# The last 64 of 576 contraction rows: from four tails of two matmuls to one stacked matmul in each of seven block products

## The chip, the cores and the metric

The kernel runs on one core of one Trainium2 chip. The time is that of one execution on the device, in microseconds (us); of several runs the median is given. Its engines work side by side, each through its own list of instructions in order: TensorE (PE, matrix products into PSUM), VectorE (DVE), ScalarE (ACT), GpSimd (POOL) and SyncE (SP, which issues most transfers). Loading a weight into TensorE is a separate instruction (PEld) that runs beside the product before it.

## The reference

A transformer block with two parallel branches on the same normalised input: attention over the positions i, i-2, ..., i-14 with 32 heads of 18 channels, and a dense ReLU layer.

```python
x = A_x                                   # [1, 2048, 576]
xn = (x - mean(x)) / sqrt(var(x) + 1e-5)
# A: q, k, v = split(xn @ wqkv)           # wqkv [576, 1728]
#    logits[w] = q[i] . k[i - 2 w] * 18 ** -0.5, w in 0..7, masked where i - 2 w < 0
#    a = (softmax(logits) . v[i - 2 w]) @ wo       # wo [576, 576]
# B: b = max(xn @ w1, 0) @ w2             # w1 [576, 4608], w2 [4608, 576]
out = x + a + b                           # float32
```

## The kernel before

**Phases and steps.** The 2048 positions are worked in two phases of 1024 (every other position each), a phase in two halves h of 512 and a half in two token blocks j of 256 (`TBN`). The first products (xn times wqkv and w1) go by weight sets of 256 columns: 18 of w1 (kind F) and 7 of wqkv (kind Q) a phase, 50 in all. A step t is one set on one half, so there are 100. Steps 0 to 3 run in a hand-written opening (`OPEN`, lines 34 to 38, run by `opening`, line 1489) as plain products (`classic`, 14 matmuls for each of four output blocks). Steps 4 to 99 (loop at line 1526) run as seven block products by Strassen and Winograd's scheme over a 2 x 2 split of the 512 first contraction rows, of the set's columns and of the half's tokens: `pstep` with P1 to P7 (line 758). The weights' combinations are B11, T1, T2, B21, T3, B22, T4, the tokens' are A-blocks (`XA`) and S1 to S4 (`XS`, made by `s_forms`).

**Precision.** An operand x is split into hi = x rounded to fp32r and lo = x - hi, and a product is hi.hi + hi.lo + lo.hi (`terms`, line 685). A block product over 256 rows is 3 terms x 2 chunks of 128 = 6 matmuls of 128 x 128 by 256 columns.

**The tail.** 576 is 512 + 64 (`DR`). The last 64 rows are no part of the blocks. Their token side `XR` holds hi in partitions 0 to 63 and lo in 64 to 127, their weight side (slot RR of the set) the same 64 rows twice, once as hi and once as lo; `rest` (line 690) issues two matmuls that give all four terms. P2, P3, P4 and P5 each end in one such tail, so a step has 7 x 6 + 4 x 2 = 50 matmuls.

**Weight sets.** `set_make` (line 513) is planned two steps ahead (line 1242) into one of two buffers (`BUF`). It sends four block transfers and two of the rest rows (the same 64 rows into both halves of the partitions) from a copy of the weights in DRAM, lets VectorE form T1 to T4 by four subtractions (c1 to c4 in `TS`), and then makes hi on ScalarE and lo on VectorE in four pairs over two slots each (`parts`, `hi_lo`). `x_load` to `x_done` and `s_forms` do the same for the tokens of the second phase; `xt_direct` for the first, straight from the transposes in PSUM (4 of 128 columns and 1 of 64 for each of 8 row blocks; in the second phase the 64 columns of two row blocks share one transpose, `x_rest`, line 1296).

**Second products.** Between the P's stand visits to the second products (`o_step`, line 951): six matmuls each, three terms by two column parts of 256 and 320, of a hidden block (`H`, in one of `NHB` = 6 buffers `HB`) with w2. The order within a step is P1, P5, P6, P2, P7, P3, P4 with the visits of the F step before dealt out behind P1, P6, P7 and P3. `h_parts` makes hi (ScalarE, with ReLU) and lo (VectorE) of a finished output block; the outputs of Q steps are turned by VectorE into one of `NST` = 4 staging buffers and go to DRAM (`q_out`).

**Attention and order.** VectorE works the attention of four units of eight heads a phase (`attention`, line 1085) as a backlog in the gaps of its other work. The order within an engine is fixed when the program is built, by a planner (`Order`) that estimates durations and gives out the operations of ScalarE and VectorE by due time. GpSimd's instructions are issued as they come: in the first phase the copies of weights into DRAM (`kept_part`, line 478), each behind a one-element copy that waits for the newest hidden block, which paces them; the reciprocal deviation of the normalisation (line 383); the mask (line 1113); and four low parts of the opening (`by_pool` of `hi_lo`).

```python
def rest(bank, s, f, xr):
    w, wd = wset(s), wide(s)
    for e in range(2):
        mm(bank[0:wd], w[:, e, RR, f, 0:wd], xr, False, e == 1)
```

Of the kernel before, what the change touches and what calls it, by code (L numbers as in the profile page):

```python
# [16 lines left out]
P = 128  # L17
NPH = 2
NI = 8
# [10 lines left out]
NHB = 6  # L30
NST = 4
# [3 lines left out]
B0 T2 B1 T3 Q000 K2 F010 F011 T4 Q011 O0101 T5 O0100 S0 O0110 T6  # L35
Q001 K3 O0111 Q010 T7 F100 F101 F110 O1000 S1 O1001 O1010 F111 M2 K4 O1011
Q111 Q100 Q110 O1100 O1101 O1111 Q101 O1110
# [3 lines left out]
T1, B11, T2, B21, T3, B22, T4, RR = range(8)  # L41
B12 = T3

PE, ACT, DVE, SP, PL = "pe", "act", "dve", "sp", "pool"
TAIL = {PE: 0.24, ACT: 0.13, DVE: 0.13}
# [3 lines left out]
class Op:  # L49


    __slots__ = ("eng", "dur", "fn", "after", "due", "end", "lag", "then", "post", "gate")

    def __init__(self, eng, dur, fn, after, due, lag=0.0):
        self.eng, self.dur, self.fn, self.due, self.lag = eng, dur, fn, due, lag
        self.after = [a for a in after if a is not None]
        self.end = None
        self.then = None
        self.post = None
        self.gate = None  # L60


class Order:
# [4 lines left out]
    def __init__(self):  # L68
        self.clk = {PE: 0.0, ACT: 0.0, DVE: 0.0, SP: 0.0, PL: 0.0}
        self.dma = 0.0  # L70
        self.gp = 0.0
        self.wait = {ACT: [], DVE: []}
# [15 lines left out]
    def give(self, op, start):  # L88
# [3 lines left out]
        if op.then:  # L92
            op.then.end = self.gp = max(self.gp, op.end) + op.then.dur
# [26 lines left out]
    def step(self, limit):  # L120
        best = None
        for eng in (ACT, DVE):
# [39 lines left out]

    def later(self, fn, n, after=(), lag=0.0):
# [17 lines left out]
    def keep(self, fn, kb, after=0.0):  # L181

        fn()
        op = Op(PL, 1.0, None, (), 0.0)
        self.clk[PL] = max(self.clk[PL], self.now(), after) + kb / 90.0
        op.end = self.clk[PL] + 3.0
        return op
# [20 lines left out]
def tile_body(ctx: ExitStack, tc: tile.TileContext, x, wqkv, wo, w1, w2, out):  # L208
# [6 lines left out]
    DR = D - KT * P  # L215
    D2 = D // 2
# [54 lines left out]
    mvp = pool("mvp", 6)  # L271
# [16 lines left out]
    XR = [keep.tile([P, 3, TBN], F32R, name=f"xr{h}") for h in range(2)]  # L288
    keep.tile([P, PADS[0]], F32, name="pad0")
    BUF = [keep.tile([P, 2, 2048], F32R, name=f"wset{b}") for b in range(2)]  # L290
    keep.tile([P, PADS[3]], F32, name="pad4")
    HB = [keep.tile([P, 2, TBN], F32R, name=f"hb{b}") for b in range(NHB)]
    WHB = [keep.tile([P, 2, TBN], F32R, name=f"oh{b}") for b in range(2)]
    keep.tile([P, PADS[3]], F32, name="pad5")
# [15 lines left out]
    def wset(s):  # L310
        return BUF[s % 2].rearrange("p e (s k c) -> p e s k c", s=8, k=2)
# [27 lines left out]

    def mm(o, l, r, start, stop):  # L340
        nc.tensor.matmul(o, l, r, start=start, stop=stop, skip_group_check=True)  # L341

    def hi_lo(hi, lo, raw, n, after, slack, behind=(), by_pool=False):

        if by_pool:
            def both():
                copy(hi, raw)
                nc.gpsimd.tensor_tensor(lo, raw, f32(hi), op=ALU.subtract)

            a = act(both, n, after, slack)  # L350
            a.then = b = Op(PL, 0.0055 * n, None, (), 0.0)
            return [a, b]
# [9 lines left out]
    TURNED = [0] * NI  # L362
# [6 lines left out]
    def normalise(i, src, after, slack, by_act=False, alloc=True):  # L369
# [8 lines left out]
        def rest():  # L378
            z["mv"] = mv = mvp.tile([P, 2], F32, name="mv")
            z["r"] = r = mvp.tile([P, 1], F32, name="rstd")  # L380
# [3 lines left out]
            if by_act:  # L384
                z["nm"] = nm = mvp.tile([P, 1], F32, name="nm")
# [14 lines left out]

        if by_act:
            MEANS[i] = b
            NORMED[i] = act(one, D + 200, [b], slack + 1.0)
        else:
            NORMED[i] = dve(two, D // 2 + 100, [b], slack + 1.0)

    def turn_pe(i, pa, pb, after=()):
        def f():
            if pa is not None:
                for k in range(KT):  # L410
                    nc.tensor.transpose(pa[:, k * P : (k + 1) * P], XN[i][:, TURNED[i] + k * P : TURNED[i] + (k + 1) * P], ident)
            if pb is not None:
                nc.tensor.transpose(pb[0:DR, 0:P], XN[i][:, KT * P : D], ident)

        return pe(f, 0.11 * ((KT if pa is not None else 0) + (pb is not None)), [NORMED[i], *after])
# [7 lines left out]
    def xt_direct(i, pa, pb, t, slack, free):  # L423
# [1152 lines left out]
```

## Time and profile before

| | us |
|---|---|
| median of 3 runs | 1114.11 (1112.05 to 1114.87) |
| the profiled execution | 1115.05 |
| its span, first to last instruction | 1113.3 |
| mean granted TensorE clock | 0.999 |

The profile is of one execution. Its page gives busy times, shares of the span and numbers of instructions of each engine; PE's busy time counts pipelined matmuls, so their spacing is read from their starts. The timeline lists runs of like instructions: start, length, engine, line of the kernel, operation, output and inputs, how many, and in brackets the idle time before with what ended it. The windows give busy times by stretch of time. A name such as bk, bkA, pm, po is a PSUM tile; wset is a weight set, xa, xs and xr are the token operands, hb a hidden block, w2t a tile of w2, sn5 and sn2 partial sums, pr, lg, kk, v, qo tiles of attention, spare the target of the pacing copies. Operations of one helper share its line: 341 is a matmul, 338 a VectorE subtraction, 335 a ScalarE copy.

### The profile page before, as it was taken

Reading aid. Unit: us, or ns where it says so; the run is one execution under the profiler, and the core shown is the slowest. Engines: PE = TensorE matmul, PEld = TensorE weight load, DVE = VectorE, ACT = ScalarE, POOL = GpSimd, SP = SyncE. Lnnn points to the kernel's source line nnn. Section 1 sums busy time; section 2 is a strip of 40 time slices with the busy share of each in tenths; the row PEclk is TensorE's granted clock in tenths of the full one; section 3 lists DMA queues with packets and bytes.
Section 4 is the critical chain, followed back from the end, with each engine's and each line's share of the span. In section 5 each row is a group of like instructions: output and inputs, shape, how many; then the busy total and the mean of one; then the engine's idle time right before and its main releaser. Section 6 shows DMA issues by size and latency. Waiting matters only on the chain.

```text
span 1113.3 us, 24046 instructions
## 1 busy us (share of the span) xinstructions
PE 1102.5 (99%) x9047; PEld 1098.6 (99%) x9047; DVE 909.0 (82%) x1749; ACT 756.2 (68%) x1561; POOL 218.3 (20%) x434
## 2 busy tenths in 40 slices
PE   9999999999999999999999999999999999999998
PEld 8998999999999999999999999999999999999998
DVE  7867999999999889955885689989998998997440
ACT  6754666566687677676794565656667766766774
POOL 4132384342554423700210000000000000000000
PEclk9999999999999999999999999999999999999999
DMA  7488488856854552463354745563625415224212
GB/s 218 105 187 199 122 216 192 184 145 169 213 158 127 163 151 84 107 158 92 110 173 93 192 93 110 122 137 83 158 76 117 107 52 141 70 56 86 78 49 86
DMA packets 329862, 144.15 MB, mean 129 GB/s; under 512 B 212097, under 2 KB 310401, under 8 KB 328513
## 3 DMA queue, kind: packets, MB, share of 16 engines
q1 hardware_dynamic: 320176, 115.76, 42.3%
q0 software_dynamic: 9408, 26.55, 8.3%
q8 instruction: 71, 1.16, 0.4%
q14 instruction: 47, 0.38, 0.1%
q10 hardware_dynamic: 160, 0.30, 0.1%
HBM read 118.42 MB, written 50.66 MB: 152 GB/s over the span
## 4 chain that ended last, share of the span: by engine, by line
PE 89%; DVE 3%; SPq 3%; DMA 2%; ACT 2%; issue 1%; POOL 0%; DVEq 0%; ACTq 0%
PE po L341 43%; PE bk L341 26%; PE pm L341 12%; PE bkA L341 7%; SPq L1061 1%; DMA qo<-qd 1%; DMA wset<-w1c 1%; DMA qo<-in_w 0%; DVE pr L1107 0%; DMA wqc<-in_wqkv 0%; DVE sn L338 0%; DVE stg L656 0%; DVE wset L338 0%; ACT x L335 0%; ACT hb L335 0%
## 5 line engine op out<-in xcount | busy, mean ns | idle before, releaser
L341 PE MATMUL po<-w2t,hb 128*128 128x256 f32 (+1 forms) x3456 | 503.5, 292 | 0.1
L341 PEld LDWEIGHTS po<-w2t,hb 128*128 128x128 f32 x3456 | 463.2, 187 | 0.4 <-DVE hb L628 0.4
L335 ACT ACTIVATE x<-po 128x576 f32<-128x576 f32 x286 | 186.3, 651 | 231.5 <-PE po L341 230.6
L341 PE MATMUL bk<-xs,wset 128*128 128x256 f32 (+1 forms) x1584 | 224.0, 277 | 0.6 <-ACT sn L335 0.6
L341 PEld LDWEIGHTS bk<-xs,wset 128*128 128x128 f32 (+1 forms) x1584 | 202.3, 187 | 0.9 <-ACT sn L335 0.8
L335 ACT ACTIVATE po<-x 128x576 f32<-128x576 f32 x286 | 187.0, 654 | 6.0
L481 POOL COPY spare<-hb 1x1 f32<-1x1 f32 x192 | 94.6, 493 | 222.8 <-ACT hb L335 222.8
L341 PE MATMUL bk<-xa,wset 128*128 128x256 f32 (+1 forms) x888 | 125.5, 278 | 1.8 <-DVE sn L338 0.9
L341 PEld LDWEIGHTS bk<-xa,wset 128*128 128x128 f32 (+1 forms) x888 | 113.7, 187 | 2.8 <-DVE sn L338 1.1
L341 PE MATMUL pm<-xs,wset 128*128 128x256 f32 (+1 forms) x720 | 102.2, 277 | 0.3 <-ACT bkA L335 0.3
L338 DVE TENSOR_TENSOR sn<-bk,sn 128x256 f32<-128x256 f32 (+1 forms) x132 | 55.2, 419 | 52.3 <-ACT hb L335 25.3
L341 PEld LDWEIGHTS pm<-xs,wset 128*128 128x128 f32 (+1 forms) x720 | 92.0, 187 | 0.7 <-ACT bkA L335 0.5
L1107 DVE TENSOR_TENSOR pr<-qo,kk 128x1152 f32<-128x1152 f32 x64 | 85.4, 1346 | 7.9 <-DMA qo<-qd 6.9
L1113 POOL TENSOR_SCALAR_AFFINE_SELECT lg<-lg 1x512 f32<-1x512 f32 x8 | 9.6, 1206 | 415.1 <-DVE lg L1110 415.1
L341 PE MATMUL bkA<-xa,wset 128*128 128x256 f32 (+1 forms) x624 | 88.3, 278 | 0.5 <-ACT bkA L335 0.5
L1110 DVE TENSOR_REDUCE lg<-pr 128x64 f32<-128x1152 f32 x64 | 85.3, 1340 | 0.2
L1139 DVE TENSOR_TENSOR pr<-lg,v 128x1152 f32<-128x1152 f32 x64 | 85.2, 1348 | 0.2
L341 PEld LDWEIGHTS bkA<-xa,wset 128*128 128x128 f32 (+1 forms) x624 | 81.4, 187 | 1.0 <-ACT bkA L335 0.7
L335 ACT ACTIVATE hb<-sn 128x256 fp32r<-128x256 f32 x140 | 57.4, 414 | 35.1 <-DVE sn L338 34.6
L341 PE MATMUL bk<-xr,wset 128*128 128x256 f32 (+1 forms) x412 | 80.4, 276 | 0.0
L338 DVE TENSOR_TENSOR wset<-ts,wset 128x512 fp32r<-128x512 f32 (+2 forms) x98 | 65.1, 665 | 10.5 <-ACT wset L335 10.3
L1146 DVE TENSOR_TENSOR pr<-pr 128x288 f32<-128x288 f32 (+1 forms) x128 | 71.4, 597 | 0.0
(156 smaller groups left out, 1551.8 us busy)
## 6 DMA issues: line engine op xcount, KB each, us to landing
w2t<-w2c SPq DMA_DIRECT2D x70, 288.0 KB, 3.3
qd<-stg SPq DMA_DIRECT2D x216, 64.0 KB, 2.0
wset<-w1c SPq DMA_DIRECT2D x105, 128.0 KB, 2.8
w1c<-in_w POOLq DMA_DIRECT2D x68, 144.0 KB, 3.4
w2c<-in_w POOLq DMA_DIRECT2D x68, 144.0 KB, 3.5
out<-x SPq DMA_DIRECT2D x16, 288.0 KB, 2.2
ts<-w1c SPq DMA_DIRECT2D x35, 128.0 KB, 2.7
wset<-w1c SPq DMA_DIRECT2D x70, 64.0 KB, 2.3
```

Of the source, the lines that this page charges most:

```text
L335: nc.scalar.activation(o, i, func)
L338: nc.vector.tensor_tensor(o, a, b, op=op)
L341: nc.tensor.matmul(o, l, r, start=start, stop=stop, skip_group_check=True)
L481: nc.gpsimd.tensor_copy(spare[0:1], f32(LATEST[-1])[0:1, 0:1])
L1061: z = send(lambda: nc.sync.dma_start(o, i.rearrange("i p c -> p i c")), cnt * 2, after)
L1107: nc.vector.tensor_tensor(pr[i], q, window(k, i), op=ALU.mult)
L1110: nc.vector.tensor_reduce(s["lg"][:, i], pr.pop(i).rearrange(heads, d=Dh), axis=AX.X, op=ALU.add)
L1113: nc.gpsimd.affine_select(out=z, in_=z, pattern=[[1, NI], [1, W], [0, HG]], compare_op=ALU.is_ge, fill=-1e9 / scale, base=1 - W, channel_m ...
L1139: nc.vector.tensor_tensor(pr[i].rearrange(heads, d=Dh), e, window(VV[u % 2], i).rearrange(heads, d=Dh), op=ALU.mult)
L1146: nc.vector.tensor_tensor(o, z[:, 0:n], z[:, n : 2 * n], op=ALU.add)
```

## The change

The contraction is split into two halves of 288 rows, each two chunks of 128 and 32 rows (`ROWS`, `XCOL`, `DH`). The 32 rows of a half belong to its blocks and go through the same seven combinations. For one block the four kinds of term are stacked in 128 partitions, 32 each: weights hi, lo, hi, 0 against tokens hi, hi, lo, lo; so one matmul (`rest`) gives the three terms that `terms` gives elsewhere, and each of the seven P's is 7 matmuls (`go`). The opening's plain products take two such matmuls, one of each half.

*Weights.* A set has seven slots of three hi and two lo chunks (`wset`). The rest rows are sent three times into 96 partitions of a new tile `RW`, whose last 32 stay zero (`thrice`), ahead of the blocks. Their combinations (`rsum`) and low parts (`rparts`, on 32 partitions) are done by GpSimd (`less`), their hi by ScalarE. `parts` now covers seven slots of two chunks instead of eight.

*Tokens.* The 2 x 32 columns of a row block are written fourfold by GpSimd (`fours`), turned by two transposes (`turn_rest`), and split by ScalarE and VectorE (`xt_rest`). Their S-forms take four more VectorE subtractions in `s_forms`, and `s_rest` writes them into the place in `XA` of the block that only the plain products read; in the second phase that block isn't made (`x_parts`). `x_rest` makes four transposes instead of one.

*Order and room.* GpSimd's work is given out by the planner like that of ScalarE and VectorE (`gp`, `keep`). The opening's list has the new steps R and another order. Hidden buffers go from 6 to 4, staging buffers from 4 to 3, pads between tiles change with them, and the planning of the last output weights of the first phase (`wo_plan`) moves one step later.

```diff
-NHB = 6
-NST = 4
+NHB = 4
+NST = 3
...
-B0 T2 B1 T3 Q000 K2 F010 F011 T4 Q011 O0101 T5 O0100 S0 O0110 T6
-Q001 K3 O0111 Q010 T7 F100 F101 F110 O1000 S1 O1001 O1010 F111 M2 K4 O1011
-Q111 Q100 Q110 O1100 O1101 O1111 Q101 O1110
+T2 R2 B0 B1 T3 K2 Q000 R3 Q001 T4 T5 F010 Q011 Q010 S0 F011 R4 O0100 R5 T6
+O0110 T7 O0101 R6 K3 R7 O0111 F100 F101 O1000 F111 S1 F110 O1010 M2 K4 Q100
+O1001 O1100 O1011 Q110 Q101 Q111 O1110 O1101 O1111
 """.split()
...
-T1, B11, T2, B21, T3, B22, T4, RR = range(8)
-B12 = T3
...
+B11, B21, B22, T1, T3, T4, T2 = range(7)
+B12 = 7
+C11, C12, C21, C22 = range(4)
+ROWS = (0, 288)
+R3 = 96
...
+    def gp(self, fn, n, after, slack):
+        op = Op(GP_, 0.0022 * n + 0.2, fn, after, self.now() + slack)
+        self.wait[GP_].append(op)
+        return op
...
+    def keep(self, fn, kb, after=(), slack=8.0):
+
+        op = Op(GP_, 0.65, fn, after, self.now() + slack)
+
+        def landed():
+            self.clk[PL] = max(self.clk[PL], op.end) + kb / 90.0
+            op.end = self.clk[PL] + 3.0
...
+        op.post = landed
...
+    DH = DR // 2
+    XCOL = [ROWS[k // 2] + k % 2 * P for k in range(KT)]
...
-        return BUF[s % 2].rearrange("p e (s k c) -> p e s k c", s=8, k=2)
+        z = BUF[s % 2]
+        cut = 21 * P
+        return (
+            z[:, 0:cut].rearrange("p (s k c) -> p s k c", s=7, k=3),
+            z[:, cut:].rearrange("p (s k c) -> p s k c", s=7, k=2),
+        )
...
+    RW = keep.tile([P, 4, P], F32, name="rw")
+    nc.gpsimd.memset(RW[R3:P], 0.0)
+
+    def thrice(src, r0):
+        return src[r0 : r0 + DH][None].to_broadcast([3, DH, src.shape[1]])
...
+    def less(o, a, b):
+        nc.gpsimd.tensor_tensor(o, a, b, op=ALU.subtract)
...
+        def fours():
+            src = XN[i].rearrange("p (q c) -> p q c", q=2)[:, :, 2 * P : 2 * P + DH]
+            nc.gpsimd.tensor_copy(XF[0][:, i % 2], src[:, :, None, :].to_broadcast([P, 2, 4, DH]))
...
+        FOURS[i] = o_.gp(fours, 256, [a, before], slack + 2.0)
...
+    def turn_rest(i, pb, after=()):
+        def f():
+            for q in range(2):
+                z = XF[0][:, i % 2, q].rearrange("p a c -> p (a c)")
+                nc.tensor.transpose(pb[:, q * P : (q + 1) * P], z, ident)
+
+        t = pe(f, 0.11 * 2, [FOURS[i], *after])
...
+    def xt_rest(i, pb, t, slack, free):
+
+        h, j, c = place(i)
...
+        b = slice(2 * j, 2 * j + 2)
+        r1 = act(lambda: copy(XR[h][:, b, c], pr), 256, [t], slack + 1)
+        r2 = dve(lambda: sub(XR[h][DR:P, b, c], pr[DR:P], f32(XR[h][DR:P, b, c])), 256, [r1], slack + 1.5)
+        r3 = act(lambda: copy(RD[h][j][:, :, c], pr), 256, [t, *free], slack + 4)
...
-        r = act(lambda: copy(XR[h][0:DR, 2], RD[h][0:DR]), TBN, RAWR[h], slack + 3)
-        ok.append([r, dve(lambda: sub(XR[h][DR:P, 2], RD[h][0:DR], f32(XR[h][0:DR, 2])), TBN, [r], slack + 3.5)])
...
+        rd = [RD[h][q // 2][:, q % 2] for q in range(4)]
+        b1 = dve(lambda: sub(rd[S1], rd[S3], rd[S1], ALU.add), TBN, [*RAWR[h], *XOK[h, 0], *XOK[h, 1]], slack + 2)
+        b3 = dve(lambda: sub(rd[S3], rd[S2], rd[S3]), TBN, [b1], slack + 2.2)
+        b2 = dve(lambda: sub(rd[S2], rd[S1], rd[S2]), TBN, [b3], slack + 2.4)
+        b4 = dve(lambda: sub(rd[S4], rd[S4], rd[S2]), TBN, [b2], slack + 2.6)
...
+    def s_rest(h, after, slack):
+
+        ops = []
+        for e in (1, 0):
+            raw = RD[h][e]
+            o = XA[h][1][:, e, 0:2]
+            k = act(lambda o=o, raw=raw: copy(o, raw), 512, [RSUM[h], *after], slack)
+            ops += [k, dve(lambda o=o, raw=raw: sub(o[DR:P], raw[DR:P], f32(o[DR:P])), 512, [k], slack + 0.8)]
+            XOK[h, 10 + (S1 if e else S2)] = XOK[h, 10 + (S1 if e else S2)] + ops[-2:]
+        return ops
...
+        for rows in range(2):
+            for v in range(1 if wd == P else 2):
+                if wd == P:
+                    d_, s_ = RW[0:R3, 2 * rows : 2 * rows + 2].rearrange("p s c -> p (s c)"), src_
+                else:
+                    d_, s_ = r[0:R3, 2 * rows + v], src_[:, v * wd : (v + 1) * wd]
+                got["r", rows] = send(
+                    lambda: nc.sync.dma_start(d_, thrice(s_, ROWS[rows] + 2 * P)), 96, [*there, *rw_free[0]], late
...
+        for rows, f, b in ((0, 0, B11), (1, 0, B21), (1, 1, B22), (0, 1, B12)) if fine else (
+            (0, 0, B11), (0, 1, B12), (1, 1, B22), (1, 0, B21)
+        ):
...
+        def rparts(a, b, c, after, slack):
+            n = wd * (b - a)
+            k = act(lambda: copy(hi[:, a:b, 2, 0:wd], r[:, c : c + b - a]), n, after, slack)
+            low = slice(DH, DR)
+            y = [k, o_.gp(
+                lambda: less(hi[low, a:b, 2, 0:wd], r[low, c : c + b - a], f32(hi[low, a:b, 2, 0:wd])), n, [k], slack + 0.5
+            )]
+            for q in range(a, b):
+                ok[q] += y
+            return y
+
+        def rsum(o, a, b, after, slack):
+            return o_.gp(lambda: less(r[:, o], r[:, a], r[:, b]), wd, after, slack)
...
+        rs = 2.0 if fine else 5.0 + y
+        r1 = rparts(B11, B21, 0, [got["r", 0]], rs)
+        e1 = rsum(0, 1, 0, r1, rs + 1.0)
+        r2 = rparts(B21, T1, 2, [got["r", 1]], rs + 0.3)
+        e3 = rsum(1, 3, 1, [e1, got["r", 1]], rs + 1.2)
+        e2 = rsum(3, 3, 0, [e3, *r2], rs + 1.4)
+        e4 = rsum(2, 2, 3, [e2], rs + 1.6)
...
+            r4 = rparts(T1, T2 + 1, 0, [e4], rs + 2)
...
+            parts(T1, T4, tw[:, 0:2], [c1, c3], [], 9 + y)
+            parts(T4, T2 + 1, tw[:, 2:4], [c4], [], 10 + y)
+            parts(B11, B22, z[:, B11:B22], [got[B11], got[B21]], [c1, c4], 11 + y)
+            parts(B22, T1, z[:, B22:T1], [got[B22]], [c2, c3], 12 + y)
+        ts_free[0] = [*ok[T1], *ok[T2]]
+        rw_free[0] = [*r4]
...
-    def rest(bank, s, f, xr):
-        w, wd = wset(s), wide(s)
-        for e in range(2):
-            mm(bank[0:wd], w[:, e, RR, f, 0:wd], xr, False, e == 1)
+    def rest(o, s, b, xr, stop=False):
+        wd = wide(s)
+        mm(o[0:wd], wset(s)[0][:, b, 2, 0:wd], xr, False, stop)
...
+        def go(o, b, xs, xr, start, more):
+            def f():
+                terms(o, slot(m, b), xs, start)
+                rest(o, m, b, xr)
+
+            return pe(f, T7, [*ok[b], *more])
...
-            def f():
-                terms(b3, slot(m, T1), sform(h, S1), True)
-                rest(b3, m, 1, XR[h][:, 1])
-
-            op = pe(f, T8, [*ok[T1], *ok[RR], *XOK[h, 10 + S1], *XOK[h, 1], *BANK[n3]])
+            op = go(b3, T1, sform(h, S1), srem(h, S1), True, [*XOK[h, 10 + S1], *BANK[n3]])
...
-
-            op = pe(f, T8, [*ok[B22], *XOK[h, 10 + S4], *BANK[n3]])
+            op = go(b3, B22, sform(h, S4), srem(h, S4), False, BANK[n3])
...
-        at(TG[2 * m] - 2, 2, wo_plan, m)
+        at(TG[2 * m] - (1 if m == WOLAST[0] else 2), 2, wo_plan, m)
...
+        XIN[i] = [send(lambda: nc.sync.dma_start(XN[i], x_v[1, i]), 295)]
...
-            for z in range(2):
-                copy(rr[h][0:DR, j, z * P : (z + 1) * P], pm[z * DR : (z + 1) * DR, 0:P])
-
-        e = act(out_, TBN + 200, [t], 0.5)
+        t = [turn_rest(i + z, pm[:, 2 * z * P : 2 * (z + 1) * P], BANK["pm"]) for z in range(2)]
+        dst = RD[h][j].rearrange("p q (z c) -> p z q c", z=2)
...
-        XOK[h, j] = hi_lo(XA[h][j][:, 0], XA[h][j][:, 1], z, 1024, RAW[h, j], 1.0)
+        k = slice(2 * j, KT)
+        z = kt4(KR[h][j])[:, k]
+        XOK[h, j] = hi_lo(XA[h][j][:, 0, k], XA[h][j][:, 1, k], z, 1024 >> j, RAW[h, j], 1.0)
...
+    def first_rest(s, raw, after, slack, behind=()):
+        hi = wset(s)[0][:, 0:4, 2]
+        low = slice(DH, DR)
+        k = act(lambda: copy(hi, raw), 512, after, slack)
+        SETREST[s] = [k, o_.gp(lambda: less(hi[low], raw[low], f32(hi[low])), 512, [k, *behind], slack + 0.8)]
```

369 lines of the change are left out of this document (190 added, 179 removed).

## The prediction

> **What bounds the kernel now.** I read the page's engine shares first, then the timeline of TensorE, then the windows of all engines.
>
> ```profile
> span 1113.3 us, 24046 instructions
> PE 1102.5 (99%) x9047; PEld 1098.6 (99%) x9047; DVE 909.0 (82%) x1749; ACT 756.2 (68%) x1561; POOL 218.3 (20%) x434
> ```
>
> TensorE stands idle for 1113.3 - 1102.5 = 10.8 us, start and end included, so the time is the number of its instructions times their spacing. A busy PE need not be PE at its peak, so I take the spacing from starts, in one step of the second phase (from its P1 at 877.01 to the next P1 at 888.94):
>
> ```profile
> 877.01 0.84 PE L341 MATMUL pm<-xa,wset 128*128 128x256 f32 x6
> 877.69 1.72 PE L341 MATMUL po<-w2t,hb 128*128 128x256 f32 x12
> 879.25 0.85 PE L341 MATMUL bk<-xs,wset 128*128 128x256 f32 x6
> 879.93 0.39 PE L341 MATMUL bk<-xr,wset 128*128 128x256 f32 x2
> 880.16 0.84 PE L341 MATMUL pm<-xs,wset 128*128 128x256 f32 x6
> ...
> 888.94 0.84 PE L341 MATMUL bk<-xa,wset 128*128 128x256 f32 x6
> ```
>
> From 877.69 to 879.25 twelve second products take 1.56 us, 0.130 each. From 879.25 to 880.16 six block matmuls and two of the xr tail take 0.91 us, 0.1138 each; the tail's two are no cheaper (0.23 for both). The whole step, 50 x 0.1138 + 48 x 0.130 = 11.93 us, is exactly the distance 888.94 - 877.01: nothing but matmuls is in it.
>
> The second engine is VectorE. Of the 35 windows of 20 us in which attention runs (160 to 480 and 640 to 1020), these are the first, the last and four of the five fullest (the fifth, 260 to 280, has 19.89):
>
> ```profile
> 160.00:180.00 20.00, 20.00 (x171) 20.00 (x171) 19.38 (x40) 10.45 (x21) 9.50 (x25) 1.00 0.83 192
> ...
> 360.00:380.00 20.00, 20.00 (x164) 20.00 (x163) 19.90 (x42) 11.94 (x25) 12.55 (x14) 1.00 0.52 147
> ...
> 440.00:460.00 20.00, 20.00 (x164) 20.00 (x164) 20.00 (x41) 13.25 (x28) 11.42 (x8) 1.00 0.25 69
> ...
> 900.00:920.00 20.00, 20.00 (x165) 20.00 (x165) 19.94 (x38) 13.23 (x28) 0.00 (x0) 1.00 0.23 65
> ...
> 980.00:1000.00 20.00, 20.00 (x164) 20.00 (x163) 19.84 (x34) 12.62 (x27) 0.00 (x0) 1.00 0.21 59
> 1000.00:1020.00 20.00, 20.00 (x165) 20.00 (x164) 18.84 (x44) 14.16 (x28) 0.00 (x0) 1.00 0.29 58
> ```
>
> The columns behind the length are busy times of PE, PEld, DVE, ACT and POOL. DVE has between 0.00 and 0.16 us left in the five fullest windows, and less than 1 us in 15 of the 35; ScalarE and GpSimd have room throughout.
>
> **The change, part by part.** *Matmuls.* Steps 4 to 99 now issue 7 x 7 = 49 instead of 7 x 6 + 4 x 2 = 50; the opening's classic products keep 14. That is 96 fewer at 0.1138: **-10.9 us**, all on the path, provided the stacked operands keep the spacing, as the xr ones did.
>
> *Transposes.* Each of 16 row blocks needs 4 + 2 = 6, 96 in all, where the opening had 5 each and the second phase 4.5: 40 + 36 = 76. The chain of waits prices one:
>
> ```profile
> 536.11 0.44 PE pm L411 x4
> 538.21 0.11 PE pm L1300
> ```
>
> Twenty more at 0.11: **+2.2 us**.
>
> *The weight parts of a set* (48 sets are made by set_make):
>
> ```profile
> L338 DVE TENSOR_TENSOR wset<-wset 128x512 fp32r<-128x512 f32 x90 | 60.5, 684 | 2.3 <-ACT wset L335 2.0
> L338 DVE TENSOR_TENSOR wset<-wset 128x256 fp32r<-128x256 f32 x4 | 1.6, 410 | 0.0
> L335 ACT ACTIVATE wset<-wset 128x512 fp32r<-128x512 f32 x90 | 55.3, 620 | 0.0
> L348 POOL TENSOR_TENSOR wset<-stg,wset 128x256 fp32r<-128x256 f32 x3 | 2.2, 764 | 0.7 <-ACT wset L335 0.7
> L348 POOL TENSOR_TENSOR w2t<-qo,w2t 128x576 fp32r<-128x576 f32 x1 | 1.4, 1424 | 0.0
> ```
>
> DVE's four low parts of 512 become three of 512 and one of 256: 0.684 - 0.410 = 0.27 us less a set, 13 us in all. ScalarE gets three more copies, at most 0.62 each (the 512 row), against 357 us in which it is idle: nothing. GpSimd gets seven instructions: the two POOL rows give (1424 - 764) / 320 = 2.06 ns an element, so about 0.50 for 128, 0.76 for 256, 1.29 for 512; four sums at 0.50 and three low parts of 128, 256 and 512 make **4.55 us a set, 218 us in all**. Low parts on 32 partitions are not in the trace; I give them the full price. GpSimd has 895 us free, so its own time costs nothing. But it shares something with DVE:
>
> ```profile
> L1113 POOL TENSOR_SCALAR_AFFINE_SELECT lg<-lg x8: 1095/1096/1560, 141.2 to 973.7; 1x512 f32<-1x512 f32 x8
> 141.17 1.56 POOL L1113 TENSOR_SCALAR_AFFINE_SELECT lg<-lg 1x512 f32<-1x512 f32 x1 [13.04 <-DVE lg L1110]
> 141.99 1.28 DVE L338 TENSOR_TENSOR w2t<-w2t 128x576 fp32r<-128x576 f32 x1 [0.23 <-ACT w2t L335]
> 793.43 1.50 POOL L1113 TENSOR_SCALAR_AFFINE_SELECT lg<-lg 1x512 f32<-1x512 f32 x1 [111.20 <-DVE lg L1110]
> 793.88 1.25 DVE L338 TENSOR_TENSOR oh<-oh 128x256 fp32r<-128x256 f32 x1
> L338 DVE TENSOR_TENSOR w2t<-w2t 128x576 fp32r<-128x576 f32 x70 | 53.0, 760 | 8.6 <-ACT w2t L335 5.9 <-DMA qd<-stg 2.1
> L338 DVE TENSOR_TENSOR oh<-oh 128x256 fp32r<-128x256 f32 x27 | 12.1, 448 | 0.6 <-ACT oh L335 0.4
> 357.20 6.73 POOL L481 COPY spare<-hb 1x1 f32<-1x1 f32 x1
> L481 POOL COPY spare<-hb x192: 173/175/7105, 45.5 to 477.6; 1x1 f32<-1x1 f32 x192
> ```
>
> Durations behind a colon are least, median and most, in ns. Twice a GpSimd select of 1.1 us met a DVE operation with two inputs in SBUF, and that one took 1.28 instead of 0.76 and 1.25 instead of 0.45: 0.52 + 0.80 us lost, over eight selects, 1.32 / (8 x 1.1) = **15% of GpSimd's time**. The other way a one-element copy of 0.17 us stood for 6.73 us behind an unbroken row of such operations. So a set costs DVE 0.15 x 4.55 - 0.27 = 0.41 us more, with one set in 1113 / 48 = 23 us 0.35 us per window. Only the five fullest windows lack that: 5 x 0.35 - (0.11 + 0.10 + 0.00 + 0.06 + 0.16) = **+1.3 us** on PE. The bounds: no meeting at all gives DVE back 13 us and costs nothing; half of GpSimd's time lost is priced under the rivals. I take the 15%, the only rate that the trace shows.
>
> The Trainium skill, "SBUF — State Buffer", section "Who interferes with whom", speaks against this change: a DVE instruction with two SBUF inputs contends with a GpSimd instruction that reads SBUF, and the second to issue fully blocks until the first is done. By that rule the loss is decided by which engine comes first, and the rows at 141.99, 793.88 and 357.20 agree with it on both sides; how often it happens to seven instructions a set no row shows, and that is what the rivals below are about.
>
> *DMA and queues.* Two rest-row transfers of 96 KB go ahead of the four block transfers on SP, in place of two of 64 KB in the middle; the blocks start two issues later. Sets are made two steps (24 us) ahead, which hides it.
>
> *Buffers.* Hidden buffers go from 6 to 4. In a step of two second-product visits after P3, then P4, P1 and the next visit, P3's output gets its buffer when both visits end (1.56 us), and is read 0.9 + 0.7 + 0.8 us later; ScalarE and DVE need about 0.8 of these 2.4. About 1 us with hand-offs is left: nothing, while DVE is on time. Staging buffers go from 4 to 3, two being filled in a step of 5.6 us or more: nothing.
>
> *Opening and turn between the phases.* The first products wait for GpSimd's low parts:
>
> ```profile
> 8.50 2.21 POOL L348 TENSOR_TENSOR wset<-stg,wset 128x256 fp32r<-128x256 f32 x3 [0.70 <-ACT wset L335]
> 12.59 1.07 PE L341 MATMUL pm<-xa,wset 128*128 128x256 f32 x8
> ```
>
> There it now makes two fourfold copies (at most the 0.76 of the 256 row each), one low part of 512 and two of 256: some 4.3 us from about 8.0, ending at 12.3, where before it ended at 10.7 and the last of them was wanted in the block at 12.59. I take **+0.8 us** for this and the later order; the bounds are +3 and, below nothing, -2.4, if these two stalls go, which hang on where a late attention load falls:
>
> ```profile
> 93.12 0.97 PE L341 MATMUL pm<-xa,wset 128*128 128x256 f32 x6 [1.53 <-DVE sn L338]
> ...
> 95.18 0.97 PE L341 MATMUL bk<-xa,wset 128*128 128x256 f32 x6 [0.85 <-DVE sn L338]
> ```
>
> **Sum**: -10.9 + 2.2 + 1.3 + 0.8 = **-6.6 us**. The profiled execution took 1115.05 us (span 1113.3), giving 1108.4 there; it lies 0.9 above the median of the runs, 1114.11, so the forecast is **1107.5 us**.
>
> **The rivals.** *All of the matmuls arrive.* GpSimd works under reductions and gaps, DVE keeps its 13 us, perhaps the stalls at 93 and 95 go: -8.7 to -11, about 1105. For it: six of eight selects met nothing. Against: DVE's full windows.
>
> *The gain is lost to the shared reads.* At 30% instead of 15% a window owes (0.30 x 4.55 - 0.27) x 0.86 = 0.94 us; 14 of the 35 windows have less, 7.0 us together, so PE pays 14 x 0.94 - 7.0 = 6.2, and -10.9 + 2.2 + 0.8 + 6.2 = -1.7: 1112.4.
>
> *Slower: DVE becomes the bound.* The same place and price, with the rate at 40%: 1.33 us a window, 22 windows short with 16.3 us between them, 12.9 on PE: +5.0, 1119 us, and 1124 at 45%. It decides from about 35%, where the sum is nothing. For it: a waiting GpSimd instruction gets in just when a one-input operation of 0.4 us begins, and holds on into the next one. Against: selects met only twice in eight.
>
> *Sets come late.* The seven GpSimd instructions are a chain with three ScalarE copies between, about 3 us to land and 7 to work in 24 us of room; one wait like the 6.73 fits in, two do not. PE then stands, in order, behind the step's first block that lacks its tail. A set late by 3 us, on five of 48, gives +15 - 6.6: 1122; on two it gives 1113. The median copy waited for nothing (175 ns), which speaks against.
>
> **How the numbers follow.** Forecast 0.34 (1105.5 to 1110.8), all arrives 0.18, lost 0.21, DVE bound 0.13, late sets 0.14 (half of it within 0.3%). A measurement here tells 0.3% from nothing, so faster is below 1110.8 and slower above 1117.5: faster 0.52, same 0.27, slower 0.21. The range 1103 to 1121 takes in all but the far ends of the last two and of the first.
>
> **What would show it.** PE with 8971 instructions and unchanged spacing; xr and xa tails one to a product; GpSimd busy some 430 us. Right: DVE's means for wset, ts and pr a few per cent up, PE idle of 10 to 15 us. Wrong: PE waiting for POOL wset, DVE's two-input means up by a tenth, long waits of PE on DVE sn or ACT hb in the full windows, or a spacing other than 0.1138.

## The result, and the profile after

The changed kernel takes 1186.42 us (median of 4 runs, 1183.51 to 1187.65), the one before 1113.08: **1.065 times as long, 95% interval 1.063 to 1.068**. Forecast was 1107.5. The page of the changed kernel, its first line and the busy times with their counts:

```profile
span 1184.1 us, 24581 instructions
PE 1125.0 (95%) x8971; PEld 1111.8 (94%) x8971; DVE 980.4 (83%) x1763; ACT 796.6 (67%) x1711; POOL 490.7 (41%) x791
```

TensorE issues the 8971 instructions foreseen, 76 fewer than before, yet it is busy 22.5 us longer and idle 1184.1 - 1125.0 = 59.1 us instead of 10.8. VectorE has 14 more instructions and 71 us more to do. Its groups with shapes kept apart (busy time, mean ns of one), in the kernel before:

```profile
L338 DVE TENSOR_TENSOR wset<-ts,wset 128x512 fp32r<-128x512 f32 x90 | 61.2, 680 | 8.5 <-ACT wset L335 8.3
L338 DVE TENSOR_TENSOR ts<-wset,ts 128x256 f32<-128x256 f32 x138 | 55.6, 412 | 6.1 <-DMA wset<-wqc 3.2 <-DMA wset<-w1c 2.3
L338 DVE TENSOR_TENSOR sn<-bk,sn 128x256 f32<-128x256 f32 x126 | 52.7, 419 | 51.5 <-ACT hb L335 25.3 <-PE bk L341 24.0 <-PE pm L1300 1.8
L1146 DVE TENSOR_TENSOR pr<-pr 128x576 f32<-128x576 f32 x64 | 46.3, 747 | 0.0
```

and in the changed one:

```profile
L359 DVE TENSOR_TENSOR wset<-ts,wset 128x512 fp32r<-128x512 f32 x90 | 77.4, 863 | 20.6 <-ACT wset L356 20.1
L359 DVE TENSOR_TENSOR ts<-wset,ts 128x256 f32<-128x256 f32 x138 | 70.3, 522 | 1.1
L359 DVE TENSOR_TENSOR sn<-bk,sn 128x256 f32<-128x256 f32 x126 | 52.3, 415 | 45.0 <-ACT hb L356 26.0 <-PE bk L365 15.5 <-ACT oh L356 2.2
L1236 DVE TENSOR_TENSOR pr<-pr 128x576 f32<-128x576 f32 x64 | 50.3, 809 | 0.0
```

The 512 row of wset<-ts,wset went from 0.680 to 0.863 us, the sums of a set from 0.412 to 0.522, the attention's pr<-pr from 0.747 to 0.809; sn<-bk, which has one input in PSUM, went from 0.419 to 0.415 us. ScalarE has waits that it did not have (total, times, longest):

```profile
ACT wset L356 <- POOL rw L362: 41.2, 20, 5.0
ACT wset L356 <- DMA rw<-w1c: 19.0, 9, 6.2
```

What such a wait does is seen in the timeline of the changed kernel, rows of GpSimd, ScalarE and TensorE together:

```profile
490.42 8.15 POOL L548 COPY spare<-hb 1x1 f32<-1x1 f32 x1
...
499.82 1.72 PE L365 MATMUL po<-w2t,hb 128*128 128x256 f32 x12
...
501.67 0.72 POOL L362 TENSOR_TENSOR wset<-rw,wset 32x128 fp32r<-32x128 f32 x1
...
503.82 1.52 POOL L362 TENSOR_TENSOR rw<-rw 128x128 f32<-128x128 f32 x3
505.37 0.63 ACT L356 ACTIVATE wset<-rw 128x512 fp32r<-128x512 f32 x1 [5.01 <-POOL rw L362]
...
507.95 3.25 PE L365 MATMUL po<-w2t,hb 128*128 128x256 f32 x12 [4.04 <-ACT po L356]
511.00 1.48 PE L365 MATMUL pm<-xs,wset 128*128 128x256 f32 x6
...
513.93 1.73 PE L365 MATMUL po<-w2t,hb 128*128 128x256 f32 x12
```

A pacing copy of one element is blocked for 8.15 us, while VectorE works off a row of instructions with two inputs in SBUF, without a break from 490.18 to 498.43. GpSimd's chain for a set stands behind this copy and two shorter ones, ScalarE stands in order at the copy that needs the chain (5.01 us), behind that copy wait the copies of po, and TensorE loses 4.04 us. Then its twelve second products take 3.25 us instead of 1.72, and the half spacing lasts until some 513.8. The windows show the granted clock, the third figure from the end:

```profile
480.00:500.00 20.00, 20.00 (x165) 20.00 (x164) 19.90 (x37) 12.68 (x29) 10.88 (x7) 1.00 0.23 68
500.00:520.00 20.00, 15.96 (x108) 15.76 (x108) 14.61 (x31) 10.49 (x22) 10.63 (x17) 0.83 0.28 79
```

Counted in TensorE's timeline, the changed kernel has 12 waits of 1.5 us or more (30.9 us together), the one before a single one (1.5 us). Its mean granted clock is 0.985 against 0.999; 0.015 x 1184 gives, as an estimate, 18 us lost to the slow stretches. Not every long wait is followed by one: behind a wait of 3.39 us, at 218.51, the clock stays at 1.00 and six matmuls take 0.97 us.

### The profile page after: what moved, and what is told of

Read it like the earlier page. It is cut to its first block, busy times and chain, and to the rows that moved or that the text cites. A ratio compares the mean times of both kernels' runs of the same rounds, so it can differ in the third digit from the quotient of the medians.

```text
span 1184.1 us, 24581 instructions
## 1 busy us (share of the span) xinstructions
PE 1125.0 (95%) x8971; PEld 1111.8 (94%) x8971; DVE 980.4 (83%) x1763; ACT 796.6 (67%) x1711; POOL 490.7 (41%) x791
## 4 chain that ended last, share of the span: by engine, by line
PE 51%; DVE 21%; POOL 7%; ACT 6%; issue 6%; DMA 5%; SPq 3%; DVEq 0%; POOLq 0%; ACTq 0%
PE po L365 25%; PE bk L365 15%; PE pm L365 7%; PE bkA L365 4%; DVE wset L359 3%; POOL spare L548 2%; DVE ts L359 2%; POOL rw L362 2%; DVE pr L1229 2%; DVE pr L1236 2%; POOL wset L362 2%; DVE hb L722 2%; DVE sn L359 1%; SPq L762 1%; ACT wset L356 1%
## 5 line engine op out<-in xcount | busy, mean ns | idle before, releaser
L365 PE MATMUL po<-w2t,hb 128*128 128x256 f32 (+1 forms) x3456 | 512.0, 295 | 13.5 <-ACT po L356 12.8
L365 PEld LDWEIGHTS po<-w2t,hb 128*128 128x128 f32 x3456 | 469.9, 190 | 15.5 <-ACT po L356 14.1
L362 POOL TENSOR_TENSOR wset<-rw,wset 32x512 fp32r<-32x512 f32 (+2 forms) x145 | 159.6, 1105 | 425.7 <-ACT wset L356 396.0
L365 PE MATMUL bk<-xs,wset 128*128 128x256 f32 (+1 forms) x1584 | 229.6, 282 | 11.2 <-ACT bkA L356 5.9
L365 PE MATMUL bk<-xa,wset 128*128 128x256 f32 (+1 forms) x1140 | 197.9, 280 | 11.5 <-DVE sn L359 8.0
L365 PEld LDWEIGHTS bk<-xa,wset 128*128 128x128 f32 (+1 forms) x1140 | 162.7, 188 | 15.0 <-DVE sn L359 8.3
L362 POOL TENSOR_TENSOR rw<-rw 128x128 f32<-128x128 f32 (+1 forms) x192 | 111.0, 578 | 13.7
L356 ACT ACTIVATE wset<-rw 128x512 fp32r<-128x512 f32 (+2 forms) x145 | 62.7, 443 | 65.7 <-POOL rw L362 41.2
L365 PE MATMUL pm<-xa,wset 128*128 128x256 f32 (+1 forms) x540 | 94.1, 281 | 7.9 <-DVE sn L359 7.8
L359 DVE TENSOR_TENSOR wset<-ts,wset 128x512 fp32r<-128x512 f32 (+2 forms) x98 | 82.4, 844 | 20.6 <-ACT wset L356 20.1
L365 PEld LDWEIGHTS pm<-xa,wset 128*128 128x128 f32 (+1 forms) x540 | 77.3, 189 | 9.3 <-DVE sn L359 9.0
```

The lines of the kernel that those rows point to most:

```text
L356: nc.scalar.activation(o, i, func)
L359: nc.vector.tensor_tensor(o, a, b, op=op)
L362: nc.gpsimd.tensor_tensor(o, a, b, op=ALU.subtract)
```

## The experiments

Rounds share their runs of the kernel before (1112.4 to 1114.1 us); ratios are to it, with their 95% intervals. The runs e2 to e5, e9, e13 and e15 leave out or alter values of the rest rows; they tell times only.

**Buffers, and GpSimd's work as a whole.**

```diff
# e1_buffers: the kernel before
-NHB = 6
-NST = 4
+NHB = 4
+NST = 3
# e2_no_gpsimd: the changed kernel, set_make
-            y = [k, o_.gp(lambda: less(hi[low, ...], r[low, ...], f32(hi[low, ...])), n, [k], slack + 0.5)]
+            y = [k, o_.gp(lambda: None, n, [k], slack + 0.5)]
-            return o_.gp(lambda: less(r[:, o], r[:, a], r[:, b]), wd, after, slack)
+            return o_.gp(lambda: None, wd, after, slack)
```

> The kernel before with four hidden buffers and three staging buffers, nothing else. If the lost buffers cost the time (theory B), a good part of the 73 us between the kernels shows here: 1130 us or more. If the loss lies with GpSimd's work (theories A and C below), 1113 to 1117, as the prediction had it.

> The changed kernel with GpSimd's four sums and its low parts of the rest rows left out of set_make; the planner's order of all other instructions stays. Theory A (VectorE and GpSimd wait for one another at SBUF, VectorE loses some 76 us) and theory C (ScalarE stands, in order, behind copies that wait for GpSimd's chain, and TensorE's granted clock drops after the stalls that follow) both expect the loss to be gone: 1104 to 1112 us, VectorE's 512 row of wset back at about 0.68 us. If buffers, the opening or the new order of the copies cost it (theory B), it stays above 1150.

e1: 1116.28 us, 1.0026 (1.0013 to 1.0038), some 2.6 us. e2: 1125.04 us, 1.0104 (1.0074 to 1.0134). GpSimd's seven instructions a set cost 61.4 of the 73 us, and 11 us above the kernel before remain without them: both theories were only partly right.

**Is it the reads, or the waits on GpSimd?**

```diff
# e3_no_chain: the sums behind the last copy of the rest rows
+        r4 = rparts(T1, T2 + 1, 0, [got["r", 0], got["r", 1]], rs + 2)
+        e1 = rsum(0, 1, 0, [*r1, *r4], rs + 2.2)
...
# e4_no_reads: each `less` of set_make
+        for _ in range(2):
+            nc.gpsimd.memset(o, 0.0)
```

> The same GpSimd instructions as in the changed kernel, but the four sums come behind the last copy of the rest rows, so ScalarE waits for none of them (the terms hold rows that are not summed). Theory C expects most of the loss to be gone: under 1130 us, with VectorE's 512 row still near 0.86. Theory A expects it to stay above 1160, since the shared reads stay.

> Each of GpSimd's subtractions in set_make becomes two fills of the same output, which read nothing, about as long; all waits between GpSimd and ScalarE stay (the rest rows' sums and low parts are not formed). Theory A expects VectorE's 512 row back at about 0.68 us and the time near 1110 to 1120. Theory C in its pure form, a chain that is too long whoever disturbs it, expects above 1150 with VectorE undisturbed; a time between would share the loss out.

e3: 1179.78 us, 1.0585 (1.0564 to 1.0606). e4: 1130.89 us, 1.0158 (1.0129 to 1.0187). VectorE's groups in e4:

```profile
L359 DVE TENSOR_TENSOR wset<-ts,wset 128x512 fp32r<-128x512 f32 x90 | 61.4, 685 | 12.8 <-ACT wset L356 12.2
L359 DVE TENSOR_TENSOR ts<-wset,ts 128x256 f32<-128x256 f32 x138 | 55.3, 414 | 1.5 <-DMA wset<-w1c 0.4
```

With all waits kept and only the reads gone, VectorE is where it was (906 us busy in all) and 55.5 us are back. By e4 against e2, and by e3 against the changed kernel, the waits alone are worth some 6 us. Neither comparison is clean: the fills of e4 take 163 us where the subtractions took 261, so its chain is shorter too, and in e3 VectorE is busy 994 us, 14 more than in the changed kernel. The shared reads are the main cause.

**The reads beside the old kernel, and the same work on VectorE.**

```diff
# e7_load_before: the kernel before, NHB = 5, when the copy of T1's high part is given out
+            nc.gpsimd.tensor_copy(spare[0:1], one)
+            for e in (0, 1, 2, 3):
+                nc.gpsimd.tensor_tensor(d[:, e], d[:, e], d[:, (e + 1) % 4], op=ALU.subtract)
+            for e in (1, 2, 4):
+                nc.gpsimd.tensor_tensor(d[l, 0:e], d[l, 0:e], d[l, 0:e], op=ALU.subtract)
# e8_half_load: the first loop alone
# e6_all_vector: the changed kernel, `sub` given to VectorE in place of `less`
```

> The changed kernel with the four sums and three low parts of a set's rest rows on VectorE in place of GpSimd. By the rows for 256 and 512 elements (0.41 and 0.68 us) that is 4 x 0.25 + 0.25 + 0.41 + 0.68 = 2.3 us a set, 108 us on top of the 906 us of VectorE when GpSimd reads nothing. Theory A: GpSimd's help cost VectorE 74 us of its time, so this comes out no better than the changed kernel, 1170 to 1210, with VectorE's 512 row at 0.68. Theory C (the hand-offs between GpSimd and ScalarE cost it) expects under 1150.

> The kernel before, with five hidden buffers to make room for a scratch tile, and beside each set the same seven GpSimd subtractions (four of 128 x 128, three on 32 rows of 128, 256 and 512) on that tile, behind a one-element copy that paces them; nothing waits for them. Theory A expects the loss without any of the change: 1160 to 1180 us, VectorE's 512 row at 0.8 us or more. If it needs the chain, the new order or the new transfers, 1113 to 1125.

> The same with the four sums of 128 x 128 alone, about 2.0 of the 4.55 us a set. Theory A, with a loss that goes with GpSimd's time: 0.45 of the loss of the full load, 1130 to 1145. If VectorE has that much time to spare before it bounds the kernel, as the prediction's sum by windows had it, less: 1113 to 1120.

e7: 1141.21 us, 1.0253 (1.0232 to 1.0274). e8: 1121.29 us, 1.0077 (1.0055 to 1.0099). e6: 1202.92 us, 1.0804 (1.0786 to 1.0822). The page of e7:

```profile
span 1139.2 us, 24455 instructions
PE 1115.5 (98%) x9047; PEld 1104.4 (97%) x9047; DVE 975.5 (86%) x1749; ACT 752.1 (66%) x1561; POOL 508.0 (45%) x819
```

VectorE loses 975.5 - 909.0 = 66.5 us to 46 x 4.55 = 209 us of such work, 32%; in e8 942.1 - 909.0 = 33 us. Half the load costs 8 us and the whole 28: below the linear share of the smaller load (0.44 x 28 = 12), as one expects of an engine with some time to spare, and just above the second range expected. e7 lies between its two ranges: nearly the same loss of VectorE's time costs the changed kernel 55 (1186.42 - 1130.89). e6 shows that this help of GpSimd is still cheaper than all the work on VectorE, then 1014 us busy, though its loss looks different: 37 of its 90 us are two waits of TensorE, 25.05 and 12.29 us (at 542.51 and 1139.94), while VectorE works off the attention that is left over near the end of each phase.

**What decides between 28 and 55?** Fewer buffers, shorter instructions, the moment:

```diff
# e10_load_buffers: e7 with NHB = 4, NST = 3
# e11_short: low parts of 256 and 512 cut into 128s
+ [less(hi[low, q : q + 1, 2, 0:wd], ...) for q in range(a, b)]
# e12_load_early: e7's load given out ahead of c1, behind the landing of the first block
+        c1.fn = lambda go=c1.fn: (load(z[0:1, B11, 0, 0:1]), go())
# e14_after_sums: ahead of a set's first low part on GpSimd
+                    nc.gpsimd.tensor_copy(spare[0:1], tw[0:1, 2, 0, 0:1])
```

> The kernel before with GpSimd's load as in e7_load_before (1141.21 us), and four hidden and three staging buffers as in the changed kernel (alone they cost 2.6 us). Theory E: fewer buffers are harmless while VectorE is on time and turn its delays into waits of TensorE when it is not, which is why the same load costs 28 us in the old kernel and 55 in the new one: 1155 to 1170. If the buffers only add up: 1141 to 1147.

> The changed kernel with GpSimd's low parts of 256 and 512 elements cut into two and four of 128, the same work in six instructions instead of two. By m1_meeting a subtraction of 512 beside VectorE's row cost VectorE 9.45 / 10 = 0.95 us and one of 128 2.73 / 20 = 0.14, so a set should cost VectorE some 0.5 us less, 23 us in all, and the time 1186 should fall by 10 to 17 us. If the loss goes with GpSimd's time whatever the length, VectorE loses a little more (GpSimd is busy four times 0.24 us longer a set) and the time is 1186 to 1195.

> The kernel before with the load of e7_load_before (1141.21 us), only paced otherwise: it starts when the set's first block has landed, and so beside VectorE's four sums of the set, as in the changed kernel, and not behind the copy that follows them. Theory F (the moment decides: GpSimd holds up the sums from which all copies of the set follow): 1155 us or more, VectorE's ts rows up from 0.46 to over 0.55 us. If only the amount of lost time decides: 1136 to 1146.

> The changed kernel with GpSimd's seven instructions of a set held back, by a one-element copy, until VectorE's four sums of the set are done. Theory F: VectorE's ts rows go back from 0.52 to about 0.42 us and the time from 1186 to under 1170. If the moment does not matter, the chain is only later: 1183 to 1200.

e10: 1146.44 us, 1.0296 (1.0264 to 1.0328): the buffers only add. e11: 1182.1 us, 1.0611 (1.0581 to 1.0641): VectorE's busy time falls from 980.4 to 967.7, half of what was expected, the time by 4 us, hardly clear of the noise; GpSimd is busy 76 us longer (566.3 us), so its chain is longer at the same time. e12: 1138.56 us, 1.0236 (1.021 to 1.0261): the load costs no more at this moment, but it hits VectorE's sums less than was meant (0.487 us, against 0.459 in e7 and 0.522 in the changed kernel). e14: 1209.53 us, 1.0863 (1.0832 to 1.0894): VectorE's sums are back at 0.416 us, but ScalarE now waits 118.9 us for GpSimd's rw, where it waited 41.2. Theory E falls. For F nothing speaks, but neither run settles it: e14 makes the chain later at the same time, and TensorE itself now waits for GpSimd's wset (23 us).

One difference stays visible: e7 has no wait of TensorE of 1.5 us or more and a granted clock of 1.000, the changed kernel 12 and 0.985. In e4, from which the 55 are counted, there are 7 such waits (15.3 us) and a clock of 0.996. So the shared reads bring 15.6 us more of long waits, and by the clocks an estimated 18 - 4.5 = 13 us more of slow stretches: 29 of the 55 us. The 27 left are about what the load costs the kernel before. That is where the difference sits; which part of the new structure lets them grow so long was not settled.

**What remains without GpSimd's work.** Counted by the second products, the same in both kernels, e2 is 9.5 us behind the kernel before at the hundredth, 9 at the 1500th and 17 after the turn between the phases.

```diff
# e5_margin: e2, the planner's landing time of the rest rows
-                    lambda: nc.sync.dma_start(d_, thrice(s_, ROWS[rows] + 2 * P)), 96, [*there, *rw_free[0]], late
+                    ... late + 4.0
# e9_rest_behind: e2, these transfers moved behind the loop over the four blocks, and last in RAWS
# e13_plain_rows: e2, 96 rows in a row in place of 32 rows three times
     def thrice(src, r0):
-        return src[r0 : r0 + DH][None].to_broadcast([3, DH, src.shape[1]])
+        r0 = min(r0, D - 3 * DH)
+        return src[r0 : r0 + 3 * DH]
```

> The changed kernel without GpSimd's sums and low parts, as in the run e2_no_gpsimd (1125.04 us), and the planner told that a transfer of rest rows lands 4 us later than it thought, so that ScalarE's copies of these rows take a later place. Theory D (ScalarE stands in order behind copies whose transfer has not landed: 24.8 us of such waits in that run, none in the kernel before) expects 1108 to 1116 us. If the remaining loss comes from the opening and the turn between the phases, it stays at 1122 to 1128.

> The changed kernel without GpSimd's sums and low parts (1125.04 us as e2_no_gpsimd), its transfers of rest rows behind the four block transfers of a set, as in the kernel before, and last among the first weights in the opening. Theory D (the rest rows' transfers, ahead on SP's queue, make the blocks and so ScalarE's copies late): the opening's 9 us and part of the turn's 8 us of lag come back, 1108 to 1117. If their place does not matter: 1122 to 1128.

> The changed kernel without GpSimd's sums and low parts (1125.04 us as e2_no_gpsimd), the transfers of rest rows reading 96 rows that follow one another in place of 32 rows three times: same bytes, same partitions, other values. Theory G (a threefold reading lands late, some 6 us after its issue in the opening, and ScalarE's next copies with it): the first product stands at 10 to 11 us instead of 13.3 and the time is 1108 to 1117. If the shape or the bytes cost it: 1122 to 1128.

e5: 1137.71 us, 1.0221 (1.0198 to 1.0245); e9: 1139.96 us, 1.0238 (1.0193 to 1.0284): a later place makes it worse, theory D as put is wrong. e13: **1107.84 us, 0.9959 (0.9944 to 0.9974)**. The opening of e2, in its timeline:

```profile
7.63 0.40 ACT L356 ACTIVATE wset<-stg 128x256 fp32r<-128x256 f32 x1
11.00 1.24 ACT L356 ACTIVATE wset<-stg 128x512 fp32r<-128x512 f32 x3 [2.97 <-DMA stg<-in_w]
12.15 0.57 ACT L356 ACTIVATE xa<-bk 128x512 fp32r<-128x512 f32 x1
...
13.26 0.73 PE L365 MATMUL bk<-xa,wset 128*128 128x256 f32 x4 [2.85 <-ACT xa L356]
```

and the same in e13:

```profile
7.73 1.53 ACT L357 ACTIVATE wset<-stg 128x256 fp32r<-128x256 f32 x4
9.17 0.58 ACT L357 ACTIVATE xa<-bk 128x512 fp32r<-128x512 f32 x1
...
10.28 0.74 PE L366 MATMUL bk<-xa,wset 128*128 128x256 f32 x4
```

ScalarE stood at the first copy of rest rows (the 128x512 one) until their transfer had landed, and the tokens' copy behind it was 3 us late. With as many bytes from rows read once each, ScalarE doesn't wait there. The transfers by themselves, and the full change with them:

```diff
# m2_landing: transfers of 96 KB, each awaited by VectorE
# e15_all_plain: the changed kernel, `thrice` as in e13
# e16_three_sends: the changed kernel
+        for q in range(3):
+            nc.sync.dma_start(dst[q * DH : (q + 1) * DH], src[r0 : r0 + DH])
```

> No part of the computation: transfers of rest rows one after the other, each awaited by VectorE: 96 rows in a row, 32 rows three times in one transfer, and three transfers of 32 rows; singly, in pairs, and in pairs ahead of a block of 128 KB. By the openings (5.96 us to landing against some 3.2) a threefold transfer takes about 2.5 us longer than a plain one, also before the block behind it lands; three transfers take a plain one's time and two issues of some 0.5 us.

> The changed kernel with all of GpSimd's work, its transfers of rest rows reading 96 rows in a row as in e13_plain_rows (other values, same work). Theory H (late transfers leave no room in a set's 24 us, so that GpSimd's reads cost twice what they cost beside the kernel before): 1107.8 + 28, 1130 to 1147 us. If the two costs only add up: 1186 - 17, 1164 to 1174.

> The changed kernel, complete, with each threefold transfer sent as three transfers of the same 32 rows. If one transfer's repeating pattern lands late, this comes out as e15_all_plain, less some 1.5 us a set of SP's time: 1132 to 1160. If reading the same rows three times is slow however it is sent: 1180 to 1195.

m2, rows of its timeline: VectorE's idle time before it sees the rows (plain, threefold, three transfers), then the block of 128 KB behind a pair of each:

```profile
7.59 0.15 DVE L29 COPY one<-raw 128x1 f32<-128x1 f32 x1 [2.03 <-DMA raw<-in_w]
...
18.75 0.15 DVE L29 COPY one<-raw 128x1 f32<-128x1 f32 x1 [4.28 <-DMA raw<-in_w]
...
32.89 0.15 DVE L29 COPY one<-raw 128x1 f32<-128x1 f32 x1 [2.77 <-DMA raw<-in_w]
...
97.08 0.15 DVE L29 COPY one<-blk 128x1 f32<-128x1 f32 x1 [3.05 <-DMA blk<-in_w]
...
113.78 0.15 DVE L29 COPY one<-blk 128x1 f32<-128x1 f32 x1 [5.91 <-DMA blk<-in_w]
...
137.29 0.15 DVE L29 COPY one<-blk 128x1 f32<-128x1 f32 x1 [4.80 <-DMA blk<-in_w]
```

The threefold pattern takes twice as long, and holds up the block behind it by 2.9 us. The Trainium skill, "DMA: Bandwidth & Descriptors", section "Rules for kernel authors", gives a reason: a leading zero-stride broadcast of c copies confines a transfer to at most c of the 16 DMA engines. These rows agree with it: the same rows in three transfers land in 2.77 us. So do m2's windows: while the second threefold transfer moves its bytes (17.00 to 18.00 us), the 16 DMA engines are busy 0.18 to 0.21 of the time, where three of sixteen would be 0.19; under a plain transfer (6.65 to 6.90) it is 0.74. With the repetition as an inner dimension, 32 rows outermost, it might go at the plain rate; that was not tried.

e15: 1175.26 us, 1.0543 (1.0521 to 1.0565): theory H falls; the two costs come near to adding up (11.2 us gained where 17.2 were to be had). e16: 1190.62 us, 1.0691 (1.0669 to 1.0712): its first product starts at 10.98 us, so the rows land in time there, but SP issues three times as many of these transfers (2.6 us for six in m2, 0.8 for two plain ones) and the block behind a pair still lands 1.75 us later than behind plain ones (4.80 against 3.05); the gain is lost again, by that or otherwise; no run tells.

**The meeting of the two engines by itself.**

> No part of the computation: rows of VectorE instructions alone and beside rows of GpSimd subtractions. If the two take turns at SBUF, instruction by instruction, a row of VectorE subtractions of 512 with both inputs in SBUF (0.68 us alone) beside GpSimd subtractions of 128 (0.5 us alone) shows about 1.2 us each on both. If VectorE's row keeps the port, its mean stays at 0.68 and the first GpSimd subtraction takes until the row ends. Subtractions with an input in PSUM and reductions (one input) keep their means beside GpSimd, and so do those of 512 beside fills, which read nothing. Mixed rows: each GpSimd subtraction starts under a one-input instruction and holds up the next two-input one.

m1, rows of its timeline, each a row of 10 or 20 instructions; DVE L32 has both inputs in SBUF, L35 one in PSUM:

```profile
5.55 14.47 DVE L32 TENSOR_TENSOR dc<-da,db 128x512 f32<-128x512 f32 x20
...
20.55 10.58 POOL L46 TENSOR_TENSOR gc<-ga,gb 128x128 f32<-128x128 f32 x20
...
31.21 16.79 POOL L46 TENSOR_TENSOR gc<-ga,gb 128x128 f32<-128x128 f32 x20
...
31.36 17.20 DVE L32 TENSOR_TENSOR dc<-da,db 128x512 f32<-128x512 f32 x20
...
49.07 14.48 DVE L32 TENSOR_TENSOR dc<-da,db 128x512 f32<-128x512 f32 x20
...
73.77 9.11 DVE L35 TENSOR_TENSOR dc<-ps,db 128x256 f32<-128x256 f32 x20
...
147.82 13.31 POOL L46 TENSOR_TENSOR gc<-ga,gb 128x512 f32<-128x512 f32 x10
...
161.21 16.27 POOL L46 TENSOR_TENSOR gc<-ga,gb 128x512 f32<-128x512 f32 x10
161.35 23.94 DVE L32 TENSOR_TENSOR dc<-da,db 128x512 f32<-128x512 f32 x20
```

Beside twenty short GpSimd subtractions VectorE's row takes 17.20 us instead of 14.47: 2.73 / 10.58 = 26% of GpSimd's own time. Beside ten of 512 it takes 23.94: 9.47 / 13.31 = 71%. Beside fills (49.07) and with an input in PSUM (73.77; 9.11 alone too) it loses nothing. Neither of the two pictures expected holds: they neither take strict turns nor does one keep the port. In the mixed rows the two-input subtractions of 512 took 0.90 us beside GpSimd and 0.69 after it when they alternated with ones that have an input in PSUM, 0.74 and 0.68 when they alternated with reductions: held up as expected, only by less.

## Why the prediction was wrong, step by step

*Matmuls (-10.9)*: right. In e13 a step of the second phase runs from 883.00 to 894.82, 11.82 us, which is 49 x 0.1138 + 48 x 0.130. *Transposes (+2.2)* and the opening's *+0.8* were not measured singly; with the matmuls and the buffers' 2.6 they make -5.3 us, and e13 lies 4.6 below the kernel before of its round (1107.84 against 1112.41).

*Buffers "nothing"*: they cost 2.6 us alone (e1).

*The shared reads (+1.3)*: the term that failed, twice over. The **rate** of 15%, from two meetings among eight selects, was 35% in the changed kernel (980.4 - 906.3 = 74 of 209 us; the 906.3 is e4's) and 32% in e7, counted on the 46 sets of full width. And the **price** of the lost time was wrong: the text let TensorE pay only what a window of 20 us lacks. At 32% that rule gives 0.86 x 0.32 x 4.55 = 1.25 us a window, 20 of the 35 windows short, 11 us; e7 measured 28, and the changed kernel 55. Time that VectorE has left within a window doesn't help an operation that is due now.

*Rivals*: "VectorE becomes the bound" named the mechanism and a rate of 35 to 45%, but with the same wrong price (up to 1124). "Sets come late" named the chain and the copy of 6.73 us; it happens (the 8.15 us copy above), yet taking the waits away brought back only some 6 us, with what was said of e3 and e4. Of the chances, half of 0.14 on top of 0.21 makes 0.28 and not 0.27; nothing rests on it.

*"Two steps ahead hides it"*, of the transfers: wrong. The threefold reading costs 1125.04 - 1107.84 = 17.2 us without GpSimd's work and 11.2 with it (e15), 3 us of it at the first product (13.26 against 10.28 us) and some 9 by the hundredth second product, at about 80 us (e2 is 9.5 us behind the kernel before there, e13 0.2). For the opening +0.8 was taken, and +3 was the bound. The number of bytes was read, the access pattern was not.

*ScalarE's copies "nothing"*: true of their time (796 us busy in e13, which is faster than the kernel before). But what stands in order on ScalarE behind a copy that waits was not named, though TensorE's order was, and not that a stretch at half spacing can follow a long wait of TensorE.

What stays open: why nearly the same loss on VectorE costs 28 us in the old kernel and 55 in the new one, that is, why the waits grow long there. e14, 23 us slower than the changed kernel though VectorE is busy 13 us less, shows that the chain's waits can cost more than 6 us. Chain (6), threefold reading (11), length of the instructions (4), buffers and moment were tried one by one, not together. No run beat both kernels but e13, which lacks part of the computation: 0.4% is what the change could bring if GpSimd's work and the threefold reading cost nothing.

## What to carry to other kernels

Work handed to GpSimd is not free where VectorE works on pairs of SBUF operands: measure the rate with a load that nothing waits for (e7, e8) before building on it. Price lost time on a nearly full engine by such a run, not by its idle time per window, and name for every new wait what stands in order behind it on that engine. Look at a transfer's outermost dimension, not only at its bytes.

## What the runs showed of the hardware

A GpSimd subtraction on 32 partitions takes about as long as one on 128: 0.73 us for 32x256 in the changed kernel with VectorE idle (at 503.01), 0.764 for 128x256 in the kernel before; in e7, beside VectorE's work, 0.65 us for 32x128 and 0.66 for 128x128. Long GpSimd subtractions disturb VectorE far more for their time than short ones (71% against 26%, m1), though cutting them in the kernel brought only 4 us. The Trainium skill, "SBUF — State Buffer", section "Who interferes with whom", names the forms that these rows show (two inputs in SBUF against a GpSimd read; no loss beside fills or with a PSUM input) and calls the port an exclusive lock; in m1 the two rows together took 17.2 us, less than the 14.47 + 10.58 of one after the other, so the measurement says a part of each instruction, not the whole. A wait of TensorE of 4.04 us was followed by half spacing for some 5.9 us (507.95 to 513.8), and one of 2.24 us in e2 (at 66 us) by six matmuls in 1.65 us instead of 0.84; behind the wait of 3.39 us at 218.51 there was no such stretch.
